# Moving six masks from VectorE to ScalarE, and leaving out the work ahead of each stage's newest tile

## The chip, the cores and the metric

One core of a Trainium2 chip. The metric is the device time of one execution in microseconds (us). The engines are TensorE (PE), VectorE (DVE), ScalarE (ACT), GpSimd (POOL) and SyncE (SP), each with a queue of its own that is worked off in order.

## The reference

```python
scores = scale * np.matmul(q, k.transpose(0, 1, 3, 2))       # B, H, S, D = 2, 8, 576, 64
kth = np.partition(scores, -32, axis=-1)[..., -32:-31]
scores = np.where(scores >= kth, scores, -1e9)
attn = softmax(scores);  x = matmul(attn, v)                 # -> 1152 tokens x 512
p = domain_probs / (domain_probs.sum(-1, keepdims=True) + 1e-09)
for e in range(4):                                           # w1: 4 x 512 x 1024
    out += p[:, e:e + 1] * (np.maximum(x @ w1[e], 0.0) @ w2[e])
h = np.maximum(np.maximum(out @ w1, out @ w2), out @ w3)     # 512 x 768 each
return h @ w_out
```

Attention over the 32 largest scores of each row, then a gated mixture of four experts, then a layer that takes the largest of three products.

## The kernel before, in words

The 1152 tokens are nine tiles of 128 rows; the eight heads are four pairs for each tile. So there are 36 pairs (tile, pair of heads), numbered from 0: pairs 8 to 11 are tile 2, 12 to 15 tile 3, 16 to 23 the tiles 4 and 5 mixed, and so on. The attention is laid out in slots, eight to a pair: `attention()` puts every step of pair n at slot 8n plus an offset from a table of options (FIRST, MIDDLE, TIGHT, SECOND, THIRD, LOOSE), and yields at the end of each slot. A pair's steps are: scores (PE) and their copy to SBUF (ACT); for each head seven VectorE instructions, four Max8 (L445) and three match-and-replace (L447), which find the 32nd largest score; the exponential (ACT); the mask; transposes of p (PE, L491 and L496) and their copies (pt, ACT); the reciprocal of the sums (guard L504 on ACT, rr L510 on DVE, rb L514 on ACT); the product with v (psv, PE), the transposed reciprocal (psr L519, its copy r L521 on ACT), the norm (xt, DVE L543); and the split of the result into a high part (xh, ACT L556) and a low part (xl, POOL L557).

The mask can be made in three ways (`mask`, L461 on). On DVE it is one instruction over 576 elements, `p = (s >= kth) * p`, with the row sums beside it (L473); its Exp has run earlier (L459). On ACT it is a steep Prelu of kth - s (L466), a new bias (L467) and the Exp with its sum (L468), which leaves the earlier Exp out. On POOL it is two instructions (pairs 0, 1, 4). `ON_ACT` lists the pairs: first heads of pairs 2 to 35, second heads of pairs 2, 5 and 6. The other second heads are masked on DVE.

The experts' matmuls are threaded between the slots. Every matrix is held as a high and a low part, and a product is three matmuls (L682 to L684). The experts run in stages over the tiles: stage 1 works on tiles 0 and 1, stage 2 on 1 and 2, stage 3 on 2 and 3, stage 4 on 3 and 4, stage 5 on 4 and 5, stage 6 on 5 alone, stages 7 and 8 on 6, 7 and 8; each takes four halves of experts. A half is a first layer (`half1`, two weights) and a second layer (`half2`, two weights, for each tile), and half2 of one half comes behind half1 of the next. Weights are loaded by SP (L212), their high part is made by ACT (whi, L271) and their low part by POOL (wlo, L277), four weights ahead of their use. At the end comes the layer of three products (`largest`).

What sets the order on PE is a planner that runs while the program is built: `clock["dve"]` counts the VectorE work placed so far (0.07 us + elements / 960 for each instruction), and after each slot the generator `products()` is advanced until `clock["pe"]` (columns / 2400) has caught up with it, plus an offset of 6. When the generator says None (it waits for a tile), the slot gets no more expert work and the clock of PE is set forward. A tile counts as ready at a fixed slot of its last pair: slot 104 for pair 11, 143 for pair 15, 191 for pair 23. When stage c is reached and its newest tile isn't ready, the kernel before does two things: with three of the tile's four pairs ready it begins the first layer of the first half on these three slices (`begun`), and if the fourth still isn't there it does the half2 that is pending (`held` keeps the weights' splitting from running further ahead meanwhile).

Of the kernel before, what the change touches and what calls it, by code (L numbers as in the profile page):

```python
# [31 lines left out]
ON_POOL = ((0, 1), (0, 1, 4))  # L32
W_AHEAD = 4
WIDE, W_FROM, W_STEP = 4, 306, 2
ON_ACT = (range(2, 36), (2, 5, 6))
STEEP = 2.0 ** 100
MASK_LATE = 2

# [2 lines left out]
TIGHT = dict(stag=3, new=1, scores=-7, at=(10, 11), guard=11, rec=11, spread=12, pv=12, turn=12, norm=13, split=13, last=14, lag=0, lag_s=1, sum=0, late=1)  # L41
SECOND = dict(TIGHT, norm=14, split=14, last=15)
THIRD = dict(stag=4, new=1, scores=-4, at=(11, 12), guard=12, rec=13, spread=13, pv=14, turn=14, norm=15, split=15, last=16, lag=0, lag_s=2, sum=0)
LOOSE = dict(stag=4, new=1, scores=-4, trans=10, pv=17, rec=15, lag=2, sum=0)

EARLY = 7
# [13 lines left out]
def kernel(  # L60
# [15 lines left out]
    B, HP, D, _, S = k.shape  # L76
# [59 lines left out]
    def bank(name):  # L136
        return pg.tile([P, 512], F32, tag="g", name=name)
# [62 lines left out]
    def whole(key):  # L200
        return key[1] in "ab" and key[0] in WHOLE
# [78 lines left out]
            w_pos["split"] += 1  # L280
            w_load_to(w_pos["split"] + 3)

    held = [None]

    def weight(key, oldest=None):

        w_split_to(w_index[held[0] or oldest or key] + W_AHEAD + 2 * whole(key))
        return w_hl[key]


# [268 lines left out]
    def attention():  # L559
# [3 lines left out]
        later, between = {}, {}  # L563

        def options(n):
            return TIGHT if n == HP - 1 else SECOND if n == 2 * HP - 1 else MIDDLE if n in (HP - 2, 2 * HP - 3, 2 * HP - 2) else FIRST if n < 2 * HP else THIRD if n == 3 * HP - 1 else LOOSE

        def at_slot(s, f, *a):
            later.setdefault(s, []).append((f, a))
# [94 lines left out]
    def tick():  # L664
        for x in list(lag):
            x.pop(0)()
            if not x:
                lag.remove(x)

    def flush():  # L670
        while lag:
            tick()
# [16 lines left out]
    def begun(ps, wt, xs, N, parts):  # L689

        for f in range(2):
            for a in parts:

                product(spread(ps[:, f * N:(f + 1) * N], xs[0][a]), [w[:, a, f * P:(f + 1) * P] for w in wt], [x[a] for x in xs], f == a == 0, False)
            yield True
# [95 lines left out]
    def experts():  # L791
        begin = {}

        def half1(c, i, u):
            tiles = STAGES[c]
            N = len(tiles) * P
            if c in WHOLE:
                ps = bank("ps1")
                w = weight((c, "a", i, u)).rearrange("p (a f) -> p a f", f=256)
                for f in range(2):  # L800
                    for a in range(KT):
                        pe(4 * P)
                        nc.tensor.matmul(ps[:, f * P:(f + 1) * P], lhsT=w[:, a, f * P:(f + 1) * P], rhs=xfull[:, a, :], start=f == a == 0, stop=f == 1 and a == KT - 1)
                    yield True
                h = hp_.tile([P, 2, 512], F32, tag="h", bufs=4, name="hfull")[:, 0, 0:2 * P]
                later(lambda: [nc.scalar.activation(out=h, in_=ps[:, 0:2 * P], func=AF.Relu), made.add(("h", c, i, u))])
                yield h
                return
            for groups in layer1(weight((c, "a", i, u)), xs_of(tiles), N, begin.pop((c, i, u), None)):
                if groups is None:  # L810
                    tick()
                    yield True
            hh, hl = hidden(N)
            count = made_h[0] = made_h[0] + 1
            if ON_POOL_H and not count % ON_POOL_H:
                raw = ms.tile([P, 2 * WIDTH], F32, tag="tm", bufs=2, name="raw")
                later(lambda: [nc.scalar.activation(out=raw[:, g], in_=ps, func=AF.Relu) for g, ps in groups],
                      lambda: [nc.scalar.activation(out=hh[:, 0:2 * N], in_=raw[:, 0:2 * N], func=AF.Copy),
                               nc.gpsimd.tensor_tensor(out=hl[:, 0:2 * N], in0=raw[:, 0:2 * N], in1=hh[:, 0:2 * N].bitcast(F32), op=ALU.subtract),  # L819
                               made.add(("h", c, i, u))])  # L820
                yield hh, hl
                return
            dve(2 * N)
            later(lambda: [nc.scalar.activation(out=hh[:, g], in_=ps, func=AF.Relu) for g, ps in groups],
                  *[lambda: None] * H_LAG,
                  lambda: [nc.vector.scalar_tensor_tensor(out=hl[:, g], in0=ps, scalar=0.0, in1=hh[:, g].bitcast(F32),
                                                          op0=ALU.max, op1=ALU.subtract) for g, ps in groups]
                  + [made.add(("h", c, i, u))])
            yield hh, hl

        outs = {}

        def half2(c, i, hs, ti):
            t = STAGES[c][ti]
            if not i % 2:
                outs[t] = po.tile([P, DM], F32, tag="o", name="ps2") if ti < 2 else bank("ps2")
            ps = outs[t]
            assert {("h", c, i, 0), ("h", c, i, 1)} <= made
            if c in WHOLE:
                for u in range(2):  # L840
                    w = weight((c, "b", i, u), (c, "b", i, 0)).rearrange("p (f n) -> p f n", f=2)
                    for f in range(2):
                        pe(4 * DM)
                        nc.tensor.matmul(ps, lhsT=hs[u][:, f * P:(f + 1) * P], rhs=w[:, f, :], start=not i % 2 and u == f == 0, stop=i % 2 == 1 and u == f == 1)
                        yield True
            else:
                yield from layer2(ps, [weight((c, "b", i, u), (c, "b", i, 0)) for u in range(2)], hs, len(STAGES[c]) * P, ti, not i % 2, i % 2 == 1)
            if not i % 2:
                return
            first = t not in accs  # L850
            if first:
                sums(t)
            later(*[lambda: None] * E_LAG, gated(ps, t, i // 2, first, c == LAST_IN[t] and i == HALVES[c][-1]))

        before = None
        for c in range(1, len(STAGES)):
            phase[0] = c
            newest = max(STAGES[c])
            if c == 1:
                i = HALVES[c][0]  # L860
                for parts in (range(HP - 2), (HP - 2,)):
                    while (newest, parts[-1]) not in x_ready:
                        yield None
                    for n, x in enumerate([(i, 0), (i, 1), (i + 1, 0), (i + 1, 1)]):
                        if not parts[0]:
                            begin[(c, *x)] = (po if n < 2 else pg).tile([P, 512], F32, tag="go"[n < 2], name="ps1")
                        yield from begun(begin[(c, *x)], weight((c, "a", *x), (c, "a", i, 0)), xs_of(STAGES[c]), 2 * P, parts)
                        flush()
            elif (newest, HP - 1) not in x_ready and c not in WHOLE:
                held[0] = c, "a", HALVES[c][0], 0  # L870
                if (newest, HP - 2) in x_ready and len(STAGES[c]) == 2:
                    i = HALVES[c][0]
                    for u in range(2):
                        w = weight((c, "a", i, u))
                        begin[c, i, u] = bank("ps1")
                        yield from begun(begin[c, i, u], w, xs_of(STAGES[c]), 2 * P, range(HP - 1))
                        tick()
                if (newest, HP - 1) not in x_ready:
                    flush()
                    for ti in range(len(STAGES[before[0]])):  # L880
                        yield from half2(*before, ti)
                    before = None
                held[0] = None
            while (newest, HP - 1) not in x_ready:
                yield None
            for i in HALVES[c]:
                hs = []
                for u in range(2):
                    for y in half1(c, i, u):
                        if y is not True:  # L890
                            hs.append(y)
                        yield True
                if i == HALVES[c][-1]:
                    x_free.update(t for t in STAGES[c] if LAST_IN[t] == c)
                if before is not None:
                    for ti in range(len(STAGES[before[0]])):
                        yield from half2(*before, ti)
                before = c, i, hs
        flush()
        yield from turned_ahead(len(STAGES))  # L900
        for ti in range(len(STAGES[before[0]])):
            yield from half2(*before, ti)
        flush()
# [193 lines left out]
```

## Time and profile before

| | |
|---|---|
| three runs | 767.23, 760.99, 768.05 us (median 767.23) |
| the profiled execution | 766.07 us, of which the span from first to last instruction is 764.2 |
| PE busy | 731.3 us, 96% of the span |
| DVE busy | 621.3 us, 81% |
| ACT busy | 488.5 us, 64% |
| POOL busy | 462.3 us, 60% |
| mean granted TensorE clock | 0.990 |

A busy time is the time in which the engine has at least one instruction under way; matmuls overlap, and their ends are modelled, so that PE can be shown busy while it is short of work. The two levels of TensorE's clock are 1.2 and 2.4 GHz, and a granted clock of 1.00 is the higher. "Idle before <-" names what ended an engine's wait.

### The profile page before, as it was taken

The numbers are of one execution on the slowest core, as the hardware profiler recorded it, in microseconds if no ns is written. First come the engines' busy times: TensorE is split into PE (matmuls) and PEld (weight loads), VectorE is DVE, ScalarE is ACT, GpSimd is POOL, SyncE is SP. The second block draws the span as 40 slices with busy tenths as digits, with TensorE's granted clock in tenths as the row PEclk, the third lists the DMA queues.
The fourth block names the chain that finished last, engine by engine and source line by source line (L and its number), as shares of the span: only waits on it lengthen the run. The fifth ranks groups of instructions, "written<-read, shape, count | busy, mean of one in ns | idle before, by whom it ended". The sixth has DMA issues, their size and how long they took to land.

```text
span 764.2 us, 13550 instructions
## 1 busy us (share of the span) xinstructions
PE 731.3 (96%) x4678; PEld 644.8 (84%) x4678; DVE 621.3 (81%) x1172; ACT 488.5 (64%) x1109; POOL 462.3 (60%) x401
## 2 busy tenths in 40 slices
PE   6899999699999998999999999999999999999998
PEld 3576788588899897988998877899998899999996
DVE  6999989959999899999999996999999954233341
ACT  4668888647888885987885756576555633433431
POOL 2514789449989885796975405677686742442520
PEclk9999999889999999999999999999999999999999
DMA  7683565425755534354452666878877752453501
GB/s 217 186 268 139 159 194 151 132 63 172 199 149 166 166 118 144 102 165 152 145 152 90 204 251 234 277 241 280 259 260 227 241 172 85 135 183 97 192 2 42
DMA packets 56485, 130.14 MB, mean 170 GB/s; under 512 B 9761, under 2 KB 23329, under 8 KB 56417
## 3 DMA queue, kind: packets, MB, share of 16 engines
q1 hardware_dynamic: 48064, 120.69, 50.2%
q10 hardware_dynamic: 8352, 8.59, 3.2%
q8 instruction: 37, 0.61, 0.3%
q14 instruction: 32, 0.25, 0.1%
HBM read 120.60 MB, written 8.65 MB: 169 GB/s over the span
## 4 chain that ended last, share of the span: by engine, by line
PE 65%; DVE 17%; ACT 8%; issue 5%; POOL 4%; DMA 0%; ACTq 0%; POOLq 0%; DVEq 0%
PE ps L682 16%; PE ps L684 16%; PE ps L683 16%; DVE m L445 8%; DVE work L447 6%; PE psv L536 2%; POOL wlo L277 2%; PE pss L425 2%; ACT whi L271 2%; PE psp L491 2%; PE pso L683 2%; PE pso L682 2%; PE psa L767 2%; PE pso L684 2%; PE pss L420 1%
## 5 line engine op out<-in xcount | busy, mean ns | idle before, releaser
L277 POOL TENSOR_TENSOR wlo<-raw,whi 128x512 fp32r<-128x512 f32 x228 | 305.7, 1368 | 107.5 <-ACT whi L271 102.8
L271 ACT ACTIVATE whi<-raw 128x1024 fp32r<-128x1024 f32 x148 | 152.6, 1056 | 33.3 <-POOL narrow L248 16.3
L682 PE MATMUL ps<-xl,whi 128*128 128x256 f32 (+1 forms) x520 | 160.5, 309 | 0.2
L684 PE MATMUL ps<-xh,wlo 128*128 128x256 f32 (+1 forms) x520 | 156.6, 301 | 0.1
L683 PE MATMUL ps<-xh,whi 128*128 128x256 f32 (+1 forms) x520 | 156.4, 301 | 0.0
L445 DVE MAX8 m<-work 128x8 f32<-128x576 f32 x216 | 155.1, 744 | 0.1
L447 DVE MATCH_REPLACE8 work<-m,work 128x576 f32<-128x576 f32 x144 | 106.6, 741 | 0.0
L682 PEld LDWEIGHTS ps<-xl,whi 128*128 128x128 f32 x520 | 98.4, 189 | 1.9 <-POOL xl L557 0.6
L683 PEld LDWEIGHTS ps<-xh,whi 128*128 128x128 f32 x520 | 97.8, 188 | 1.3 <-issue 0.7
L684 PEld LDWEIGHTS ps<-xh,wlo 128*128 128x128 f32 x520 | 97.6, 188 | 0.3 <-POOL wlo L277 0.3
L277 DVE TENSOR_TENSOR wlo<-raw,whi 128x1024 fp32r<-128x1024 f32 x34 | 55.1, 1622 | 48.8 <-ACT whi L271 35.9
L682 PE MATMUL ps<-wlo,h 128*128 128x512 f32 x160 | 67.7, 423 | 7.5 <-POOL wlo L277 7.5
L248 POOL TENSOR_TENSOR narrow<-narrow,raw 128x256 int32<-128x256 int32 x48 | 47.1, 982 | 38.0 <-DVE narrow L245 13.0
L684 PE MATMUL ps<-whi,h 128*128 128x512 f32 x160 | 64.3, 402 | 2.0 <-POOL h L819 2.0
L683 PE MATMUL ps<-whi,h 128*128 128x512 f32 x160 | 64.0, 400 | 0.0
L432 ACT ACTIVATE s<-pss 128x288 f32<-128x288 f32 x144 | 51.2, 401 | 14.6 <-PE pss L420 11.3
L445 DVE MAX8 m<-s 128x8 f32<-128x576 f32 x72 | 53.8, 748 | 5.5 <-ACT s L432 5.5
L447 DVE MATCH_REPLACE8 work<-m,s 128x576 f32<-128x576 f32 x72 | 53.3, 741 | 0.0
L494 ACT ACTIVATE pt<-psp 128x512 f32<-128x512 f32 x72 | 42.7, 594 | 12.2 <-PE psp L491 11.9
L491 PE MATMUL psp<-ident,p 128*128 128x128 f32 x288 | 43.8, 281 | 5.4 <-POOL p L477 4.1
L684 PE MATMUL ps<-x2h,wlo 128*128 128x384 f32 x144 | 48.7, 338 | 0.0
L682 PE MATMUL ps<-x2l,whi 128*128 128x384 f32 x144 | 48.7, 338 | 0.0
(118 smaller groups left out, 1616.1 us busy)
## 6 DMA issues: line engine op xcount, KB each, us to landing
raw<-in_w_dram SPq DMA_DIRECT2D x112, 512.0 KB, 4.2
raw<-narrow SPq DMA_DIRECT2D x36, 512.0 KB, 3.4
whole<-in_w_dram SPq DMA_DIRECT2D x30, 512.0 KB, 5.9
raw<-in_m_dram SPq DMA_DIRECT2D x36, 256.0 KB, 4.3
narrow<-narrow ACTq DMA_DIRECT2D x48, 128.0 KB, 4.3
kraw<-in_k_dram SPq DMA_DIRECT2D x16, 288.0 KB, 4.5
qraw<-in_q_dram SPq DMA_DIRECT2D x48, 64.0 KB, 3.8
raw<-in_mo_dram SPq DMA_DIRECT2D x12, 256.0 KB, 4.1
```

The source lines that it names most:

```text
L248: nc.gpsimd.tensor_tensor(out=out.bitcast(I32), in0=out.bitcast(I32), in1=last, op=ALU.add)
L271: nc.scalar.activation(out=hi, in_=raw, func=AF.Copy)
L277: on.tensor_tensor(out=lo[:, x], in0=raw[:, x], in1=hi[:, x].bitcast(F32), op=ALU.subtract)
L425: nc.tensor.matmul(ps[:, 0:SH], lhsT=l, rhs=r, start=i == 0, stop=i == len(mm) - 1)
L432: nc.scalar.activation(out=s[:, h, :], in_=halves[h][:, 0:SH], func=AF.Copy)
L445: nc.vector.max(m[:, 8 * r:8 * r + 8], src)
L447: nc.vector.match_replace(out=self.w[j], in_to_replace=m[:, 8 * r:8 * r + 8], in_values=src, imm_value=NEG)
L491: nc.tensor.transpose(ps[:, r * P:(r + 1) * P], self.p[:, part, part * TAIL + r * P:part * TAIL + (r + 1) * P], ident)
L494: return lambda: [nc.scalar.activation(out=d, in_=ps.rearrange("p (r n) -> p r n", r=NR), func=AF.Copy), self.did.add(("pt", part))]
L682: nc.tensor.matmul(ps, lhsT=lh, rhs=rl, start=first, stop=False)
L683: nc.tensor.matmul(ps, lhsT=lh, rhs=rh, start=False, stop=False)
L684: nc.tensor.matmul(ps, lhsT=ll, rhs=rh, start=False, stop=last)
```

## The change

The second heads of pairs 8, 9, 10, 12, 13 and 14 (the 9th to 11th and the 13th to 15th) get their mask from ACT instead of DVE. These six pairs take a new table of options, BOTH, in place of LOOSE: the same slots, with the second head's mask at offset 12 instead of 11, the first head's at 8 instead of 9, and the transposes of p where they were (13 and 14). And the block that gives a stage work while its newest tile isn't ready is taken out with its variable `held`, for all stages but the first (whose own branch stays): such a stage yields None until the tile is there.

```diff
-ON_ACT = (range(2, 36), (2, 5, 6))
+ON_ACT = (range(2, 36), (2, 5, 6, 8, 9, 10, 12, 13, 14))
...
+BOTH = dict(stag=4, new=1, scores=-4, at=(13, 14), pv=17, rec=15, lag=2, sum=0, late=1)
 LOOSE = dict(stag=4, new=1, scores=-4, trans=10, pv=17, rec=15, lag=2, sum=0)
...
-    held = [None]
-
     def weight(key, oldest=None):
-        w_split_to(w_index[held[0] or oldest or key] + W_AHEAD + 2 * whole(key))
+        w_split_to(w_index[oldest or key] + W_AHEAD + 2 * whole(key))
         return w_hl[key]
...
-            return ... else THIRD if n == 3 * HP - 1 else LOOSE
+            return ... else THIRD if n == 3 * HP - 1 else BOTH if n in ON_ACT[1] else LOOSE
...
-            elif (newest, HP - 1) not in x_ready and c not in WHOLE:
-                held[0] = c, "a", HALVES[c][0], 0
-                if (newest, HP - 2) in x_ready and len(STAGES[c]) == 2:
-                    i = HALVES[c][0]
-                    for u in range(2):
-                        w = weight((c, "a", i, u))
-                        begin[c, i, u] = bank("ps1")
-                        yield from begun(begin[c, i, u], w, xs_of(STAGES[c]), 2 * P, range(HP - 1))
-                        tick()
-                if (newest, HP - 1) not in x_ready:
-                    flush()
-                    for ti in range(len(STAGES[before[0]])):
-                        yield from half2(*before, ti)
-                    before = None
-                held[0] = None
             while (newest, HP - 1) not in x_ready:
                 yield None
```

## Rows read from the trace of the kernel before

**Rows 1.** The page: busy time of the engines; the largest group of Max8

```profile
PE 731.3 (96%) x4678; PEld 644.8 (84%) x4678; DVE 621.3 (81%) x1172; ACT 488.5 (64%) x1109; POOL 462.3 (60%) x401
...
L445 DVE MAX8 m<-work 128x8 f32<-128x576 f32 x216 | 155.1, 744 | 0.1
```

**Rows 2.** Windows: length, then busy PE, PEld, DVE, ACT, POOL, clock, DMA, GB/s

```profile
88.18:129.32 41.14, 38.13 (x286) 34.64 (x287) 36.56 (x78) 33.40 (x76) 35.09 (x30) 1.00 0.56 167
129.32:166.17 36.85, 29.06 (x191) 24.44 (x191) 27.78 (x53) 19.33 (x51) 18.37 (x19) 0.86 0.44 127
166.17:205.28 39.11, 37.28 (x275) 33.72 (x274) 38.05 (x79) 32.88 (x73) 36.04 (x33) 1.00 0.54 149
205.28:307.12 101.84, 98.86 (x780) 88.64 (x779) 95.92 (x205) 80.72 (x195) 80.10 (x71) 0.98 0.50 152
307.12:764.20 457.08, 452.21 (x2724) 409.92 (x2722) 342.87 (x586) 262.30 (x554) 257.75 (x212) 1.00 0.53 175
```

**Rows 3.** Timeline of DVE (start, us, instruction): masks of pairs 8, 10, 14

```profile
106.66 0.81 DVE L473 SCALAR_TENSOR_TENSOR p<-s,m,p 128x576 f32<-128x576 f32 x1
...
134.73 5.58 DVE L473 SCALAR_TENSOR_TENSOR p<-s,m,p 128x576 f32<-128x576 f32 x1
...
197.08 1.92 DVE L473 SCALAR_TENSOR_TENSOR p<-s,m,p 128x576 f32<-128x576 f32 x1 [0.20 <-ACT p L459]
```

**Rows 4.** Timeline of POOL, 133 to 158

```profile
133.96 2.54 POOL L277 TENSOR_TENSOR wlo<-raw,whi 128x512 fp32r<-128x512 f32 x2
...
137.16 2.54 POOL L277 TENSOR_TENSOR wlo<-raw,whi 128x512 fp32r<-128x512 f32 x2
...
152.26 4.97 POOL L277 TENSOR_TENSOR wlo<-raw,whi 128x512 fp32r<-128x512 f32 x4
```

**Rows 5.** Timeline of ACT, 141 to 158

```profile
141.87 0.31 ACT L556 ACTIVATE xh<-xt 128x128 fp32r<-128x128 f32 x1 [5.51 <-DVE xt L543]
...
157.40 0.60 ACT L494 ACTIVATE pt<-psp 128x512 f32<-128x512 f32 x1 [4.39 <-PE psp L491]
```

**Rows 6.** Timeline of PE, 153 to 166

```profile
153.59 0.79 PE L682 MATMUL ps<-wlo,h 128*128 128x512 f32 x1 [5.36 <-POOL wlo L277]
154.18 0.63 PE L683 MATMUL ps<-whi,h 128*128 128x512 f32 x1
...
159.41 0.60 PE L491 MATMUL psp<-ident,p 128*128 128x128 f32 x4
...
160.48 0.40 PE L682 MATMUL ps<-wlo,h 128*128 128x512 f32 x1
...
163.22 0.38 PE L533 MATMUL psv<-pt,v_last 128*128 128x128 f32 x2
...
165.27 0.28 PE L682 MATMUL ps<-xl,whi 128*128 128x256 f32 x1
```

**Rows 7.** Timeline of DVE, 150 to 166

```profile
150.88 0.75 DVE L445 MAX8 m<-s 128x8 f32<-128x576 f32 x1
...
158.13 0.17 DVE L510 RECIPROCAL rr<-rs 128x2 f32<-128x2 f32 x1 [3.26 <-ACT rs L504]
...
165.31 0.29 DVE L543 TENSOR_TENSOR xt<-psv,r 128x128 f32<-128x128 f32 x1 [4.98 <-ACT r L521]
```

**Rows 8.** Groups of ACT instructions: count, then busy us and mean ns

```profile
L466 ACT ACTIVATE s<-s,m 128x576 f32<-128x576 f32 x37 | 28.9, 782 | 0.0
...
L467 ACT ACTIVATE nb<-m,nb 128x1 f32<-128x1 f32 x37 | 11.0, 296 | 0.0
```

**Rows 9.** Timeline of PE, 294 to 300

```profile
294.68 0.50 PE L682 MATMUL ps<-wlo,h 128*128 128x512 f32 x1 [1.90 <-POOL wlo L277]
...
296.53 0.63 PE L683 MATMUL ps<-whi,h 128*128 128x512 f32 x1
...
299.50 0.29 PE L425 MATMUL pss<-kT,ql 128*128 128x288 f32 x1
```

More of the change, by code (lines that the diff above doesn't have):

```diff
@@ L565, in options @@
         def options(n):
-            return TIGHT if n == HP - 1 else SECOND if n == 2 * HP - 1 else MIDDLE if n in (HP - 2, 2 * HP - 3, 2 * HP - 2) else FIRST if n < 2 * HP else THIRD if n == 3 * HP - 1 else LOOSE
+            return TIGHT if n == HP - 1 else SECOND if n == 2 * HP - 1 else MIDDLE if n in (HP - 2, 2 * HP - 3, 2 * HP - 2) else FIRST if n < 2 * HP else THIRD if n == 3 * HP - 1 else BOTH if n in ON_ACT[1] else LOOSE
         def at_slot(s, f, *a):
```

## Prediction

> **What bounds the kernel now.** I read the page first, for the shares of the engines: TensorE (PE) has work for 96% of the span, VectorE (DVE) for 81% [rows 1]. A busy PE is not always a PE at its peak, so the second view is the table of windows, cut where pairs begin (the first Max8 of pair n's first head is the start of slot 8n: pair 8 at 88.18, 11 at 129.32, 13 at 166.17, 16 at 205.28, 24 at 307.12). The reader is to see two things in it [rows 2]. From 307.12 on PE is busy 452.2 of 457.1 us and DVE is not: the end of the kernel is a stretch in which PE works without a break, and all matmul work that isn't done before it is done there. And before it there is one bad stretch: between 129.32 and 166.17 PE is busy only 29.06 of 36.85 us, at a granted clock of 0.86, while DVE, ScalarE (ACT) and GpSimd (POOL) sag with it. The windows on either side of it lose 3.0, 1.8 and 3.0 us of PE.
>
> Since the change leaves every matmul in place, the span is PE's work plus what PE loses by waiting and by its low clock. So I ask where that loss falls and what the change does to it.
>
> The third view is the timeline of that stretch, engine by engine. In order of time: DVE's mask of pair 10's second head starts at 134.73 and takes 5.58 us, where the same instruction takes 0.81 at 106.66 [rows 3]. POOL has work all that time, two weight halves from 133.96 and two more from 137.16 to 139.70, with a query split between them [rows 4]; the mask ends 0.6 us after POOL's run does. DVE is late, so ACT sits 5.51 us before it gets xt [rows 5], POOL is kept waiting by ACT, and the next weight's low half starts only at 152.26 [rows 4]. PE has meanwhile got to the early second-layer products that the planner put in front of stage 2: it waits 5.36 us for that low half, and then runs at the lower of its two clock levels (1.2 GHz), where a product takes 0.63 us at 154.18 against 0.40 us at 160.48 [rows 6]. The transposes of pair 11 stand behind these products in PE's queue, so ACT waits 4.39 us for one of them [rows 5], and DVE waits 3.26 us for rs and 4.98 us for r [rows 7]. Four slots (100 to 104) take from 150.88 to 166.17, 15.3 us, where four slots of DVE work are some 5.9 us (eight instructions of 0.74 [rows 1], pair 12's).
>
> **What this stretch costs PE.** Idle: 36.85 - 29.06 = 7.8 us. A mean clock of 0.86 of 36.85 us is 10.3 us at half rate, of which 5.4 were idle; the 4.9 us that were busy lost half of it, 2.5 us. Together 10.3 us.
>
> **Part 1, masks to ACT.** Six DVE masks go. In this trace they took 12.2 us in all (0.81, 1.64, 5.58, 1.03, 1.25 and 1.92; the first, the third and the last are in [rows 3]). ACT gets the Prelu (0.78) and the new bias (0.30); its Exp was there before and only moves. That is 1.1 us a head and 6.5 in all [rows 8]. ACT has room: 33.4 of 41.1, 19.3 of 36.9 and 32.9 of 39.1 us in the three windows, which become 35.6 (two heads), 20.4 (one) and 36.1 (three) [rows 2].
>
> What does PE get of the 12.2? Of the long one, much: it starts the row of waits above. Of the five others (6.7 us), at most what PE loses in the windows at 88.18 and 166.17, 3.0 + 1.8 = 4.8 us; at the least nothing, because ACT's 6.5 us come in the same windows and ACT stands at 92% of the last one. I take nothing: there ACT is the nearer bound after the change.
>
> The lengthening itself is the thing to look at, for the mask reads two SBUF operands while POOL reads SBUF: by the rows the 0.81 us become 1.6 to 5.6 when POOL is working. The page "SBUF — State Buffer" of the Trainium skill (section "Who interferes with whom") says that a DVE instruction with two SBUF inputs and a POOL instruction that reads SBUF shut each other out, for the whole of the instruction that came first. The trace agrees in kind. As worded it would allow one POOL instruction (1.3 us) of delay, 2.1 us for such a mask; the row shows 5.58, through several POOL instructions that follow each other, and with only 2.1 to win there the sum would be up to 3.5 us higher, 764.7.
>
> The six masks also leave the planner's DVE clock, 0.67 us each by its formula. Three of them lie before slot 98, three between 104 and 139. The planner hands PE that much less expert work beside the attention, 2.0 us twice; it is done later, at no cost as long as PE is then dense.
>
> **Part 2, no work ahead of the newest tile.** The planner's clocks, followed through the code, enter the removed block three times: stage 2 at slot 98 (last pair of tile 2 due at 104), stage 3 at slot 139 (due at 143) and stage 4 at slot 182 (due at 191). At stages 2 and 4 it puts the 24 products of half2 of the last expert half there, 24 x 0.228 = 5.5 us of PE (twelve of them take from 160.48 to 163.22 [rows 6]); at stage 3 the 36 products of a first layer begun on three slices, half as wide, some 4 us.
>
> After the change stage 1 ends 2.0 planner microseconds later, near slot 100, and PE gets attention alone until slot 104. The 5.5 us of half2 come after stage 2's first half. With the 2.0 us of the later masks stage 3 is reached about 7 us late, at slot 144, with its tile there: no wait. Stage 4 is reached at about 187 and waits until 191; in the kernel before, the planner was empty over the same four slots, after its early half2. So from slot 191 on PE is 5.5 us of work behind, and that is paid at the end. It has its return only if the attention reaches slot 191 more than 5.5 us sooner. In terms of PE's loss this comes to the two waits:
>
> Wait of stage 2. Without the early products DVE runs slots 100 to 102, six instructions of 0.74, in 4.4 us; then norm, xh and xl stand in line, about 1 us as estimated from the 0.3 to 0.5 us of other small instructions here: x is there some 5.5 us after slot 100 began. PE's attention work in between is what it did from 159.41 to 160.48 and from 163.22 to 165.27, 3.1 us [rows 6]. That leaves 2.4 us idle. The row of the other early half2 shows that even 1.90 us of idleness is followed by the lower clock: a product takes 0.63 us at 296.53, and only at 299.50 is the stretch over; some 1.5 us lost, half of the time between [rows 9]. Together I take 4.5 us; the bounds are 2 (PE is late anyway, and DVE waits for it) and 15.3 - 3.1 = 12.2 (the four slots take as long as now).
>
> Wait of stage 4. Now PE loses 1.9 us idle and 1.5 to the clock there, 3.4 [rows 9]. After: four slots of DVE work, 5.9 us, less 3.1 us of attention work as at stage 2, is 2.8 idle, and the same 1.5 make 4.3. I take 0.9 us more loss; the bounds are 3.4 less (PE is late and never waits) and 5.5 more (all that the early products filled).
>
> Nothing is added to SP's or POOL's queue: the weight loads and splits follow the products they serve, and while PE waits POOL can only catch up.
>
> **Sum.** The profiled execution took 766.07 us (span 764.2 and 1.9 around it), 1.2 below the median of 767.23. 766.1 - 10.3 + 4.5 + 0 (five masks) + 0.9 (stage 4) = 761.2.
>
> **Rivals.** *The gain goes elsewhere (no change).* Masks that stay on DVE (pair 11's second head at slot 99, pairs 15 and up) can meet a POOL run as pair 10's did; one stall of 5 us in front of an empty PE gives the same row of waits back. Or ACT, in order and with 36.1 us of work in 39.1, hands its weight halves to POOL later, and PE waits for wlo as it does now. For it: wlo is what ended two of PE's longest waits [rows 6, 9]. Against it: of the other 29 masks none took 2 us. 764 to 771 us.
>
> *The waits cost their whole length (slower).* The early products fill a wait whose length DVE, ACT and the chain of pair 11 set; taking them out shortens nothing, and PE stands still for their 5.5 us at stage 2 and again at stage 4. It decides if pair 11's first transposes still come more than 3 us after its mask. Price: up to 11 us against what the pair 10 stall gives back, 766.1 + 5.5 to 11 = 772 to 777. For it: PE paid a low clock after both its gaps. Against it: the transposes came late because they were queued behind the wlo wait [rows 5, 6]. On the clock the page "TensorE: Matmul & The Clock Gate" of the Trainium skill (section "What's actually happening") speaks for this rival: the low rate is the resting state and only work lifts it, so an emptier PE pays twice. The rows of both gaps agree.
>
> *More than forecast.* The five other masks give their 4.8 us too and ACT keeps up: 751 to 756 us.
>
> **How the numbers follow.** About 1% is what a measurement of this kernel can tell from no change; of 767.23 that is 759.6 and 774.9. Chances: forecast (756 to 765) 0.50, more than forecast 0.10, no change 0.22, slower 0.18. Below 759.6 lie about half of the forecast case and all of the larger gain: 0.35. Above 774.9 lies most of the slow case: 0.15. Within 1%: 0.50. The range 753 to 772 leaves out most of the slow case and a piece of the largest gain, 0.2. The likeliest case's own range is 756 to 765.
>
> **What the profile after would show.** Right: no DVE mask near 5 us between pairs 8 and 14; 43 Prelus on ACT where there are 37 [rows 8]; slots 100 to 104 in 6 to 8 us; PE losing 4 to 5 us around the start of stage 2, not 10; pair 13 beginning some 13 us sooner than 166.17; the end after the last pair longer by about 5.5 us of matmuls. Wrong: a long mask of pair 11 or 15, PE waiting for wlo at stage 2's first products, or PE idle for over 8 us between slots 98 and 104.

## The result

The changed kernel takes 755.58 us (median of 4 runs, 753.14 to 761.89), the kernel before 767.09 us in the same measurement. The ratio is 0.988 (95% interval 0.9843 to 0.9918): 1.2% faster, against 0.8% forecast. The profiled execution took 755.31 us, its span is 753.5.

The page of the changed kernel, busy time of the engines, answers to [rows 1]:

```profile
PE 728.9 (97%) x4678; PEld 643.6 (85%) x4678; DVE 604.8 (80%) x1160; ACT 495.1 (66%) x1127; POOL 457.7 (61%) x401
```

The windows below are cut at the same pairs as [rows 2], with one cut more: pairs 8, 11, 12 (second head, which is slot 100), 13, 16, 24 and the end. Columns: length, then busy PE, PEld, DVE, ACT and POOL with their instructions, granted clock, DMA share, GB/s. First the changed kernel:

```profile
88.08:126.75 38.67, 35.22 (x254) 31.54 (x255) 33.30 (x72) 32.43 (x78) 32.35 (x29) 0.96 0.57 172
126.75:146.41 19.66, 19.66 (x149) 17.55 (x149) 17.42 (x38) 17.04 (x42) 13.12 (x13) 1.00 0.53 164
146.41:152.03 5.62, 5.26 (x45) 4.44 (x44) 5.38 (x16) 2.98 (x11) 0.46 (x1) 1.00 0.50 93
152.03:188.66 36.63, 33.09 (x240) 29.34 (x239) 32.81 (x72) 33.61 (x80) 30.45 (x28) 1.00 0.43 123
188.66:289.88 101.22, 101.22 (x823) 92.48 (x823) 96.81 (x205) 82.98 (x198) 84.32 (x75) 1.00 0.55 166
289.88:753.50 463.62, 458.21 (x2747) 414.54 (x2745) 338.99 (x589) 266.19 (x559) 262.14 (x217) 1.00 0.54 175
```

And the two of the kernel before that lie between the start of pair 11 and that of pair 13:

```profile
129.32:150.88 21.56, 16.47 (x123) 13.96 (x122) 21.56 (x40) 13.83 (x37) 11.56 (x12) 0.95 0.57 161
150.88:166.17 15.29, 12.58 (x68) 10.48 (x69) 6.22 (x16) 5.50 (x16) 6.81 (x7) 0.73 0.26 79
```

What to see: slots 100 to 104 take 5.62 us instead of 15.29, at full clock. By the start of pair 13 the changed kernel is 14.1 us ahead (152.03 against 166.17), at pair 16 16.6, at pair 24 17.2. From there to the end it needs 463.62 us where 457.08 were enough: the matmuls that had been put off make PE busy for 6.0 us more there (458.21 against 452.21), and 0.5 us more are lost. That leaves 10.7 us of the span.

The wait of stage 2, on PE of the changed kernel, from the last products of stage 1 to the first of stage 2:

```profile
147.37 0.39 PE L683 MATMUL ps<-whi,h 128*128 128x512 f32 x1
147.60 1.03 PE L490 MATMUL psp<-ident,p 128*128 128x128 f32 x8
...
149.63 0.49 PE L532 MATMUL psv<-pt,v_last 128*128 128x128 f32 x2 [0.36 <-ACT pt L498]
...
151.65 0.29 PE L424 MATMUL pss<-kT,qh 128*128 128x288 f32 x1
151.78 0.28 PE L681 MATMUL ps<-xl,whi 128*128 128x256 f32 x1
```

PE is still at stage 1's products when pair 11's last mask ends (146.4 on DVE), goes on to the transposes of pair 11, and starts stage 2 at 151.78. It loses 0.36 us. Half2, which stood here before, comes later.

### The profile page after: what moved, and what is told of

Its sections match the earlier page's. It is cut to its first block, busy times and chain, and to the rows that moved or that the text cites. A ratio compares the mean times of both kernels' runs of the same rounds, so it can differ in the third digit from the quotient of the medians.

```text
span 753.5 us, 13557 instructions
## 1 busy us (share of the span) xinstructions
PE 728.9 (97%) x4678; PEld 643.6 (85%) x4678; DVE 604.8 (80%) x1160; ACT 495.1 (66%) x1127; POOL 457.7 (61%) x401
## 4 chain that ended last, share of the span: by engine, by line
PE 81%; ACT 8%; DVE 7%; issue 2%; POOL 1%; DMA 0%; ACTq 0%; POOLq 0%; DVEq 0%
PE ps L681 18%; PE ps L682 18%; PE ps L683 18%; PE psv L535 4%; PE pss L424 3%; DVE m L444 3%; PE psp L490 3%; DVE work L446 3%; ACT whi L272 2%; PE ps L843 2%; PE ps L802 2%; PE pso L682 2%; PE pso L681 2%; PE psa L766 2%; PE pso L683 2%
## 5 line engine op out<-in xcount | busy, mean ns | idle before, releaser
L278 DVE TENSOR_TENSOR wlo<-raw,whi 128x1024 fp32r<-128x1024 f32 x34 | 53.3, 1567 | 57.3 <-ACT whi L272 45.1
L249 POOL TENSOR_TENSOR narrow<-narrow,raw 128x256 int32<-128x256 int32 x48 | 44.5, 927 | 40.1 <-DVE narrow L246 12.2
L681 PE MATMUL ps<-wlo,h 128*128 128x512 f32 x160 | 66.0, 413 | 0.6 <-POOL wlo L278 0.6
L683 PE MATMUL ps<-whi,h 128*128 128x512 f32 x160 | 63.2, 395 | 0.9 <-POOL h L818 0.9
L682 PE MATMUL ps<-whi,h 128*128 128x512 f32 x160 | 62.9, 393 | 0.0
L682 PE MATMUL ps<-x2h,whi 128*128 128x384 f32 x144 | 48.6, 337 | 0.0
```

The costliest lines, as they stand in the source:

```text
L249: nc.gpsimd.tensor_tensor(out=out.bitcast(I32), in0=out.bitcast(I32), in1=last, op=ALU.add)
L278: on.tensor_tensor(out=lo[:, x], in0=raw[:, x], in1=hi[:, x].bitcast(F32), op=ALU.subtract)
L681: nc.tensor.matmul(ps, lhsT=lh, rhs=rl, start=first, stop=False)
L682: nc.tensor.matmul(ps, lhsT=lh, rhs=rh, start=False, stop=False)
L683: nc.tensor.matmul(ps, lhsT=ll, rhs=rh, start=False, stop=last)
```

## Experiments

The theories. A: the loss came from DVE masks that collide with POOL, pair 10's above all (the prediction's story). B: the six masks count alike, as VectorE load. C: the early products standing in front of pair 11's transposes cost the time. Others came up on the way and are named where they do; from e5 on an expectation calls A the theory that it tests itself. Each ratio is against the kernel before, measured beside it; that kernel's own median was 763.6 us beside e1 to e4, 762.9 beside e5 to e8, 767.6 beside e9 and e10 and 767.4 beside e11 and e12, so ratios are compared, not medians of different groups.

### e1: the masks alone

```diff
-ON_ACT = (range(2, 36), (2, 5, 6))
+ON_ACT = (range(2, 36), (2, 5, 6, 8, 9, 10, 12, 13, 14))
```

BOTH is the one of the change; `held` and its block stay.

> The six masks on ScalarE as in the change, the work ahead of the newest tile kept as before. If the loss came from masks that meet a GpSimd run (theory A), or from VectorE's load as such (B): most of the gain, 755 to 759 us against 767. If it came from the early products that stand in front of pair 11's transposes (C): 764 to 767, with TensorE still waiting some 5 us for wlo at stage 2.

Measured: 757.21 us, ratio 0.9899 (0.9865 to 0.9933). As A and B had it, the masks bring most of the change's gain. But the four slots of the kernel before are all there. The window from slot 100 to pair 13, then ACT, POOL and PE in it:

```profile
147.29:162.21 14.92, 10.52 (x54) 8.49 (x53) 5.47 (x16) 6.07 (x15) 6.66 (x6) 0.77 0.40 110
```

```profile
150.19 0.63 ACT L819 ACTIVATE h<-raw 128x512 fp32r<-128x512 f32 x1
150.73 1.99 ACT L272 ACTIVATE whi<-raw 128x1024 fp32r<-128x1024 f32 x2
```

```profile
150.90 1.26 POOL L820 TENSOR_TENSOR h<-raw,h 128x512 fp32r<-128x512 f32 x1 [4.27 <-ACT h L819]
152.12 4.97 POOL L278 TENSOR_TENSOR wlo<-raw,whi 128x512 fp32r<-128x512 f32 x4
```

```profile
148.44 0.60 PE L492 MATMUL psp<-ident,p 128*128 128x128 f32 x4
153.45 0.80 PE L683 MATMUL ps<-wlo,h 128*128 128x512 f32 x1 [4.41 <-POOL wlo L278]
```

There is no long mask here, and PE still waits 4.41 us. The two weights of the early products get their high part at 150.73 and their low part from 152.12 on, when PE has been standing at the product since 149. Nothing was late: the program asks for them only there. `weight()` has four weights split, counted from the older of the two in use; in the order of loading, the two weights of the half2 that is pending come behind the first two of the next stage, so they are the first that lie beyond the four. While `half2` follows `half1`, as elsewhere, that is soon enough. Put in front of the stage, it isn't.

### e2: the block alone

```diff
-    held = [None]
...
-            elif (newest, HP - 1) not in x_ready and c not in WHOLE:
-                ...
```

The whole block goes, as in the change; all masks stay as they were.

> Only the work ahead of the newest tile is taken out, all masks stay where they were. Up to slot 98 the program is that of before. A: pair 10's mask is long again (about 5 us) and the time is 762 to 767. B: 766 to 770, since VectorE has as much to do and TensorE less in front of its waits. C: the mask may be long, but the transposes of pair 11 come at once, and the time is 755 to 759.

Measured: 763.0 us, ratio 0.9965 (0.9933 to 0.9998). The window from slot 100 to pair 13, and pair 10's mask ahead of it:

```profile
150.87:156.15 5.28, 4.54 (x41) 3.94 (x41) 5.28 (x16) 2.42 (x9) 0.46 (x1) 1.00 0.01 3
```

```profile
134.72 5.58 DVE L472 SCALAR_TENSOR_TENSOR p<-s,m,p 128x576 f32<-128x576 f32 x1
```

The mask is as long as before, and the four slots take 5.28 us. With e1 this takes the prediction's chain of causes apart: the 15 us belong to the early products, the long mask to itself. The time lay in A's span, but not for A's reason. C has the mechanism right and the price wrong: removing 10 us of stall brings only 0.35%. In the profile pair 13 begins 10.0 us sooner than before and pair 24 7.3 us sooner (299.83), and from there the end takes 5.3 us longer (462.37 us; PE busy 456.55 against 452.21), because the 24 products are done later. The 2.7 us lost between pairs 13 and 24 are not explained.

### e3: pair 10's mask alone

```diff
-ON_ACT = (range(2, 36), (2, 5, 6))
+ON_ACT = (range(2, 36), (2, 5, 6, 10))
```

Pair 10 takes the table BOTH with it, so its first head's mask comes one slot sooner as well.

> Only pair 10's second head is moved to ScalarE, everything else as before. A: that one mask was the cause, 757 to 761 us, no wait of 5 us for wlo at stage 2. B: one sixth of the relief, 764 to 766. C: 765 to 767.

Measured: 759.4 us, ratio 0.9933 (0.9904 to 0.9961); A's number. The stretch from pair 11 to slot 100 goes from 21.56 to 16.26 us, the 5 us of the mask. The next stretch doesn't follow, and PE still waits 3.2 us for wlo there (5.36 before), where A had no long wait:

```profile
145.79:159.32 13.53, 10.82 (x54) 8.71 (x55) 5.58 (x15) 4.96 (x14) 6.66 (x6) 0.75 0.34 100
```

So of the masks' 1.0% pair 10 has about two thirds, and the five others the rest, 0.3% or 2.6 us; the intervals of e1 and e3 overlap.

### e4: pair 10's mask one slot later

```diff
-                two(b0 + 7 + late, pr.mask, j, ...)
+                two(b0 + 7 + late + (n == 10 and j == 1), pr.mask, j, ...)
```

> Pair 10's second head stays on VectorE, but its mask is issued one slot (two instructions) later; nothing else is changed. A: it falls at another place in GpSimd's run and takes 0.8 to 2.5 us, so the time is 758 to 763. B and C: nothing changes, 765 to 768.

Measured: 766.81 us, ratio 1.0049 (1.0016 to 1.0081): a miss for A. The mask is short, as A said, and the time is not:

```profile
138.61 1.54 DVE L473 SCALAR_TENSOR_TENSOR p<-s,m,p 128x576 f32<-128x576 f32 x1
```

```profile
149.21:164.82 15.61, 12.90 (x68) 10.62 (x69) 6.22 (x16) 5.49 (x16) 6.81 (x7) 0.78 0.26 77
```

Pair 13 starts at 164.82, only 1.35 us sooner than before: pair 11 began 1.8 us later than before (DVE waits 2.8 us for a product of PE ahead of it, against 1.2), the mask costs 1.5 where ScalarE's costs DVE nothing, and the stall of slots 100 to 104 is whole. The late start of pair 11 doesn't come from the edit. It lies ahead of the moved mask: in both traces PE waits 1.7 to 1.8 us at 121, but here it then runs at the lower clock (granted clock 0.85 from 120.00 to 131.14), in the trace of before at the higher (1.00). The same matmul, here and then before:

```profile
124.00 0.63 PE L684 MATMUL ps<-whi,h 128*128 128x512 f32 x1
```

```profile
123.71 0.39 PE L684 MATMUL ps<-whi,h 128*128 128x512 f32 x1
```

So the trace of e4 is a weaker witness against A than its time.

### e5: the early products' weights first

The block and the masks of e1, but stage 2's early products get their weights in time: they are put in front of that stage's first weights in the order of loading.

```diff
             for c in range(1, len(STAGES)):
                 for i in HALVES[c]:
+                    swap = c == 2 and i == HALVES[c][0]
+                    if swap:
+                        yield b(*before, 0)
+                        yield b(*before, 1)
                     yield a(c, i, 0)
                     yield a(c, i, 1)
-                    if before:
+                    if before and not swap:
...
-                held[0] = c, "a", HALVES[c][0], 0
+                held[0] = (before[0], "b", before[1], 0) if c == 2 else (c, "a", HALVES[c][0], 0)
```

> The six masks on ScalarE and the work ahead of the newest tile kept, as in e1_masks_only; but the two second-layer weights that stage 2's early products need stand before that stage's first weights in the order of loading and splitting, so that they are split well ahead. If TensorE's wait at stage 2 is for weights that are split only then (theory A): no wait of 4 us for wlo, the four slots 100 to 104 take 8 to 11 us instead of 14.9, and the time is 752 to 755 us against 757 of e1. If ScalarE's and GpSimd's lateness sets it whatever the order (D): 756 to 758 and the same 15 us.

Measured: 747.88 us (746.93 to 749.25), ratio 0.98 (0.9741 to 0.9858), 1% below e1 and better than A expected. The window from slot 100 to pair 13, and PE's only wait in it:

```profile
144.00:152.66 8.66, 8.31 (x54) 6.31 (x53) 5.47 (x15) 5.99 (x15) 5.00 (x5) 1.00 0.35 62
```

```profile
149.00 0.50 PE L689 MATMUL ps<-whi,h 128*128 128x512 f32 x1 [0.28 <-POOL h L824]
```

The early products are made, pair 13 begins at 152.66, 0.6 us behind the changed kernel, and the end isn't lengthened (459.20 us from pair 24 on, e1 459.28). This settles what the stall was: late weights, by their place in the order. Of the 10.5 us between the spans of e1 and e5 (755.6 and 745.1) 6.3 lie in these four slots. Another 2.7 lie in pairs 8 to 11 (36.48 us against 39.20, at a granted clock of 1.00 against 0.96); that these come from the order isn't shown.

### e6: the changed kernel, pair 10's mask back on DVE

```diff
-ON_ACT = (range(2, 36), (2, 5, 6, 8, 9, 10, 12, 13, 14))
+ON_ACT = (range(2, 36), (2, 5, 6, 8, 9, 12, 13, 14))
```

> The changed kernel with pair 10's second head back on VectorE; the other five stay on ScalarE. If that mask meets GpSimd's run again (A): 4 to 6 us for the mask, and 759 to 761 us against 755.6. If the six masks count alike, as VectorE load (B): 756 to 757. If the collision hangs on where the mask falls, and the others have shifted it: 1 to 2 us for the mask and 755 to 757.

Measured: 758.85 us, ratio 0.9926 (0.989 to 0.9962), against 0.988 of the changed kernel. The mask, again on DVE:

```profile
136.94 1.10 DVE L472 SCALAR_TENSOR_TENSOR p<-s,m,p 128x576 f32<-128x576 f32 x1
```

It doesn't collide for long, and the kernel loses some 3.5 us all the same (0.0046 of 767; the intervals of the two ratios overlap). Neither A (a long mask) nor B (one sixth, under 2 us) foresaw that. The profiled execution, the longest of the ten, is of little help: it is 3.4 us behind the changed kernel already at pair 8 (91.47 against 88.08), ahead of the edit. From there to the end it needs 2.1 us more, 2.0 of them between pairs 11 and 13 (27.29 against 25.28). With e4 this speaks against the length of this one mask as the only price of leaving it on DVE, but doesn't settle it.

### e7: the planner's clock as if DVE still made the masks

```diff
             if self.on_act[j]:
                 ...
+                if j == 1 and self.n > 7:
+                    dve(S)
```

> The changed kernel, but the planner's VectorE clock still counts 0.67 us for each second-head mask that has moved to ScalarE, so TensorE gets as much expert work beside the attention as when VectorE made them. If the moved masks gain by relieving VectorE and GpSimd's rival accesses (A, B): 754 to 757, as the changed kernel. If they gain because TensorE's queue holds less in front of the attention (E): most of it goes, 759 to 763.

Measured: 758.09 us, ratio 0.9936 (0.9899 to 0.9973): between the two expectations, and nearer to A and B's. Two windows, pairs 8 to 11 and 16 to 24:

```profile
88.20:129.10 40.90, 38.89 (x286) 34.64 (x287) 34.45 (x74) 35.39 (x82) 34.63 (x31) 1.00 0.58 171
189.62:293.99 104.37, 101.05 (x808) 90.92 (x807) 99.14 (x207) 82.15 (x196) 82.93 (x73) 1.00 0.52 151
```

With the masks on ACT but the expert work placed as if they weren't, pairs 8 to 11 take 40.90 us, as before (41.14), and not 38.67. That isn't yet the loss, for from pair 11 to 13 e7 is the shorter one (21.55 us against 25.28) and pair 13 begins at 150.65, 1.4 us ahead of the changed kernel. It is lost after that: 38.97 us against 36.63 from pair 13 to 16, and 104.37 against 101.22 from 16 to 24. Part of what the masks bring comes through the planner: PE is handed less to do beside the attention. By the two ratios (0.9936 against 0.988) that part is some 4 of the 9 us that the change gains; their intervals overlap.

### e11: less expert work, masks as before

```diff
-SHARE, AHEAD = (1.0, 1.0, 1.0), 6
+SHARE, AHEAD = (1.0, 0.96, 0.96, 1.0), 6
```

> The kernel before with all its masks on VectorE and its work ahead of the newest tile; only the planner gives TensorE 4% less expert work for each microsecond of its VectorE clock in stages 1 and 2, which puts stage 2 at slot 99 and stage 3 at slot 144, as the six masks' leaving does in e1_masks_only. If about half of the masks' gain came from TensorE's shorter queue (E): 761 to 764 us against 767. If it all came from VectorE's relief: 766 to 769.

Measured: 762.76 us, ratio 0.9979 (0.9944 to 1.0015). Inconclusive: the interval holds no change and a gain of half a per cent. The profiled execution shows a gain that is lost again. Pair 24 begins at 299.03, 8.1 us sooner than before (pair 10's mask has moved too, and takes 1.10 us), and the rest takes 10 us longer than in the kernel before: PE is busy for 3.6 us more (455.82 against 452.21) and idle for 6.4 more (11.25 against 4.87).

```profile
299.03:766.10 467.07, 455.82 (x2717) 411.00 (x2717) 347.74 (x589) 263.00 (x555) 260.13 (x215) 1.00 0.53 173
```

Most of the added idle time has a place. The mask of another pair meets a long run of POOL, and PE is idle for 4.48 us around it, waiting for xt and for pt:

```profile
370.21 7.72 DVE L473 SCALAR_TENSOR_TENSOR p<-s,m,p 128x576 f32<-128x576 f32 x1
```

```profile
366.00:396.00 30.00, 25.52 (x180) 22.14 (x179) 30.00 (x51) 18.41 (x45) 19.31 (x19) 1.00 0.41 126
```

So a long mask does cost PE time, as A had it, without a wait for wlo behind it. The profiled execution took 767.86 us; seven of the ten took 761.7 to 763.9, and whether these have such a mask isn't known. And e11 changes two things at once, PE's queue and the places where masks fall.

How much of the masks' gain is DVE's relief and how much PE's shorter queue is not settled; e7 puts the second at some 4 us of 9, with overlapping intervals.

### e8: the product with v one slot later

```diff
-BOTH = dict(stag=4, new=1, scores=-4, at=(13, 14), pv=17, ...)
+BOTH = dict(stag=4, new=1, scores=-4, at=(13, 14), pv=18, ...)
```

> The changed kernel with the product with v of the six pairs one slot later (18 instead of 17), so that ScalarE's copies of p are further ahead of it. TensorE waits 8.5 us in eight places for these copies in the changed kernel. If these waits are its largest loss left (A): 751 to 754 us. If the wait only moves to the next instruction, or the later norm holds up VectorE: 755 to 758.

Measured: 751.06 us (750.44 to 751.5), ratio 0.9835 (0.9786 to 0.9884). PE's longest wait in the changed kernel, and then the same wait here:

```profile
PE psv L532 <- ACT pt L498: 8.5, 8, 2.1
```

```profile
PE psv L532 <- ACT pt L498: 4.3, 6, 1.4
```

The numbers are us in total, times, longest. The wait is 4.2 us shorter in all, and by the two ratios (0.9835 against 0.988, with overlapping intervals) the kernel gains 3.4. It would be natural to call the wait the price of the masks on ACT, where Prelu, bias and Exp stand in the queue ahead of the copies of p. The other traces don't bear that out. The kernel before, and then e2, which has all six masks on DVE and only the block out:

```profile
PE psv L533 <- ACT pt L499: 4.6, 5, 1.4
```

```profile
PE psv L532 <- ACT pt L498: 8.6, 10, 1.5
```

e1, with the six masks on ACT and the block kept, has 5.2 us of it. The wait grows where the block is out and hardly where the masks move.

### e9, e10 and e12: the order by itself, and combinations

e9 takes the order of e5 alone, with nothing else changed from the kernel before; e10 is e5 with `pv=18`, and e12 is e5 with `SHARE = (1.0, 0.96, 0.96, 1.0)`. The edit of e9:

```diff
+                    swap = c == 2 and i == HALVES[c][0]
+                    if swap:
+                        yield b(*before, 0)
+                        yield b(*before, 1)
                     yield a(c, i, 0)
                     yield a(c, i, 1)
-                    if before:
+                    if before and not swap:
...
-                held[0] = c, "a", HALVES[c][0], 0
+                held[0] = (before[0], "b", before[1], 0) if c == 2 else (c, "a", HALVES[c][0], 0)
```

> The kernel before with all its masks and its work ahead of the newest tile; only the two weights of stage 2's early products stand first, as in e5_weights_first. If those products lost their time to weights that were split too late (A): the same 9 us that this order gave beside the masks on ScalarE, 753 to 757 us against 763 to 767, with slots 100 to 104 in 8 to 10 us and pair 10's mask as long as it falls. If pair 10's long mask sets the wait whatever the order (F): 762 to 765.

> e5_weights_first with the product with v of the six pairs one slot later, as in e8_pv18. If the two losses are apart: 743 to 746 us. If TensorE is dense in these slots already, and the wait for ScalarE's copies (4.5 us in four places in e5) hides under it or moves: 747 to 750.

> e5_weights_first (masks on ScalarE, the early products' weights first) with the planner's 4% less in stages 1 and 2 on top. If TensorE's queue is still too full there (E): 744 to 747 us. If the six masks have already taken what there was to win, the tail is longer by what is put off: 748 to 751.

e9: 761.04 us, ratio 0.9908 (0.9872 to 0.9943). That is a gain, but a smaller one than A expected (753 to 757). In its profiled execution pair 25's mask takes 5.96 us (1.53 in the trace of before), so only the part ahead of pair 24 is read:

```profile
150.80:161.66 10.86, 10.07 (x58) 8.44 (x59) 6.12 (x16) 5.39 (x16) 6.83 (x7) 0.84 0.49 134
```

The four slots take 10.86 us, with pair 10's mask at 5.58 just before them. The order of two weights brings about as much as all six masks, and a long mask in front doesn't bring the stall back. e10: 747.44 us, ratio 0.9743 (0.9726 to 0.9759), the same time as e5 on other runs: in e5 PE has no idle time left between pairs 13 and 24 (34.67 of 34.67 and 98.57 of 98.57 us busy), and the copies' wait is hidden there. e12: 751.88 us, ratio 0.9814 (0.9753 to 0.9874): nothing is won over e5, and the end is longer by what is put off. First the window from slot 100 to pair 13, and an early product of stage 2 in it, then the end:

```profile
142.93:149.13 6.20, 6.20 (x47) 5.19 (x45) 5.37 (x15) 2.93 (x10) 0.46 (x1) 1.00 0.82 192
```

```profile
142.91 0.48 PE L687 MATMUL ps<-wlo,h 128*128 128x512 f32 x1
```

```profile
284.34:751.00 466.66, 460.48 (x2763) 416.49 (x2761) 342.81 (x589) 268.52 (x560) 263.21 (x217) 1.00 0.53 174
```

466.66 us from pair 24 on, against 459.20 in e5 (PE busy 460.48 and 454.66). Followed through its code, the planner of e12 still makes stage 2's early products, but reaches stage 4 only at slot 191, when its tile counts as ready, so that stage 4 makes none. e5 and e10 are faster than both kernels of this case, with the work in front of the stage kept and not taken out.

## Why the prediction came out as it did

The sign and the frame held: the span is PE's work plus what PE loses, the loss sat between pairs 11 and 13, and what the attention gains is partly paid back after pair 24. Pair 13 was to begin some 13 us sooner and did by 14.1; the end was to be 5.5 us longer and is 6.5; slots 100 to 104 were to take 6 to 8 us and take 5.62; there are 43 Prelus (x43). None of the signs of being wrong shows: the longest mask left on DVE takes 1.74 us. The total of 761.2 was 5.6 us too high, and the time lies just under the likeliest case's own range, in the wide one. That it came so near is in part luck. The change takes out the long mask and the early products together, so the 10.3 us went whichever of the two had made them, and the errors of the sum have both signs.

*Terms of the sum that were mis-sized.* The wait of stage 2 was put at 4.5 us of loss, 2.4 idle and the rest clock; it costs 0.36, at full clock. The bound below, 2 ("PE is late anyway"), was the better guess and still too high. The reasoning let PE arrive when the planner's clock does. In the trace PE is behind the planner: it makes stage 1's last products at 147.4, when the slots without expert work have begun. Two things can put it there, and which of them does isn't shown. The planner lets PE's clock run ahead of DVE's by its offset of 6, and it counts 0.107 us for a matmul of 256 columns and 0.213 for one of 512, where the trace of before has 0.118 (22 steps from 128.32 to 130.91) and 0.228 (12 from 160.48 to 163.22 [rows 6]) from start to start. A wait that the planner sees isn't one that PE sees. The same holds for stage 4, which was to lose 0.9 us more than now: PE is busy for all of the 101.22 us from pair 16 to pair 24, where it had lost 3.0 us idle and another 1.0 to the clock [rows 2, 9]. (The planner, too, had less to wait: followed through the changed code it reaches stage 3 at slot 147, not 144, and stage 4 at 189, not 187.) Together these two are 4.1 and 4.9 us. Against them stand 1.2 us more loss in pairs 8 to 11 (3.45 us idle and 0.8 to the clock, for 3.0), 1.7 in pairs 13 to 16 (3.54 for 1.83) and 0.5 after pair 24. 761.2 - 4.1 - 4.9 + 3.4 = 755.6.

*The step that failed.* The prediction had pair 10's long mask start the row of waits that made slots 100 to 104 slow. e1 and e3 have no long mask and 14.9 and 13.5 us there; e2 has the long mask and 5.3 us. The stall was made by the early products: their weights were split only when PE stood before them (e1), and put in time the stall is gone (e5). The rows that looked like a chain, ACT late by 5.51 us [rows 5], then POOL, then PE [rows 4, 6], were one thing after another, not one from another: without the long mask the next weight's low half still starts only at 152.12 (e1). What is right of it is that a long mask costs PE some 5 us where it stands (21.56 us to 16.26 in e3; 4.48 us of idle PE in e11). The rival "the waits cost their whole length" fell for the same reason: what it named as its test, transposes that come more than 3 us after their mask, doesn't happen once nothing is queued in front of them. The rival "the gain goes elsewhere" didn't come true in the changed kernel, but e11 shows that it can.

*Parts.* "Five masks: 0" was too low: e1 against e3 gives them 2.6 us, with overlapping intervals. Pair 10's mask is worth 5 us from the kernel before (e3) and some 3.5 in the changed one (e6). Whether the collision is the whole reason isn't shown: kernels with a short mask in its place (1.54 us in e4, 1.10 in e6) weren't as fast, but both traces also lost time ahead of that mask. "Done later, at no cost" for the expert work that the planner puts off was too low as well: e7 makes it a gain of some 4 us, with overlapping intervals. ACT was feared as the nearer bound. PE waits 8.5 us for its copies of p, half of which one slot more takes away (e8), but by e2 and e1 that wait comes with the removed block and not with the masks.

*The two halves of the change.* Masks alone 0.9899, removal alone 0.9965, both 0.988. The removal gives 2.7 us without the masks, near the edge of what these runs can tell, and 1.5 with them, inside it. It ends a stall of 10 us by giving up the work in front of the wait; e5 ends it and keeps the work, and is 0.8% better by the two ratios, whose intervals just meet.

## What to carry to other kernels

Before taking filler work out of a wait, look at what the filler itself waits for: here work was brought forward, and the operands that it needs were not, so the filler stalled the queue that it was to fill. And a wait in a planner that runs ahead of time is a wait of the engine only if the engine is where the planner has it: here PE came late to the slots that the planner left empty, and 0.36 us of the wait was left.

## What the runs showed of the hardware

A DVE mask (128 x 576, two operands in SBUF) takes 0.79 to 0.82 us when POOL is idle at its start: all 30 such masks in the profiles of before, after and e2. With a POOL instruction under way at their start 54 masks took 0.81 to 5.58 us, on average 1.4 (the prediction read 1.6 to 5.6). The page "SBUF — State Buffer" of the Trainium skill (section "Who interferes with whom") says that such instructions and POOL's reads of SBUF exclude each other for a whole instruction. Most of these rows agree, with 0 to 1.1 us on top. Pair 10's mask doesn't: 5.58 us, in before, e2 and e9 alike, until 0.6 us after the last of several POOL instructions in a row. It isn't alone. Masks of other pairs took 3.91 us at 324.23 in e4, 3.93 at 317.01 in e3, 5.96 at 333.37 in e9 and 7.72 at 370.21 in e11, and each of them, too, ended 0.6 us after POOL's run did; in the trace of before no mask but pair 10's took 2 us. So an edit that moves the masks by a little can make another one long. Why DVE got in between POOL's instructions elsewhere and not there stays open.

An equal wait of PE is not always followed by the same clock: 1.74 us of it at 121 were followed by a granted clock of 1.00 in before, 1.76 us at the same place by the lower level in e4, and pair 11 began 1.8 us later there.

The same program varied by more than expected: 760 to 770 us for the kernel before, so that differences under half a per cent were out of reach even with ten runs (e2, e4 and e11 touch that edge).
